# First channel product of batches 2 and 3 in eleven half-block products in place of twelve

## The chip, the cores and the metric

The kernel runs on one core of a Trainium2 chip, in one launch. The metric is the device time of one execution in microseconds (us). The core has TensorE (matrix products, written PE in the profile, with its weight loads as PEld), VectorE (DVE), ScalarE (ACT), GpSimd (POOL) and SyncE (SP), each with an instruction stream of its own that it works through in order; they wait for each other by semaphores. TensorE writes its results to `P`, the accumulation memory of 8 banks of 128 x 512 fp32 numbers; VectorE and ScalarE fetch them from there.

## The reference

Two stages, for 4 batches of 768 tokens and 8 heads of width 48 (together 384 channels). The first is a recurrence over the tokens of each head: the state S (48 x 48) gives y_t = q_t S, and then takes in beta_t k_t (v_t - S k_t), with k normed. The second is a mixer on x = y of all heads:

```
h = transpose(x) @ U @ V          (over the tokens, rank 32)
u = x + transpose(h)
out = u + max(u @ w_ch1, 0) @ w_ch2      (384 -> 1536 -> 384)
```

All is fp32. The inputs q, k, v, beta and the weights come as 64-bit floats and are converted on the chip.

## The kernel before

The recurrence is done in chunks of 64 tokens. Each batch has two units n of 6 chunks; a unit's triangular systems are solved on VectorE (`blocks`, a chain of pairs of operations at L596 and L602), and joined and applied by small products on TensorE (L505 to L888). Its outputs land in `X`.

The mixer of a batch is done in three groups i of 256 tokens (`GT`). `front(b, i)` adds the low-rank part for two tiles of 128 tokens (a product with `v_sb` at L1054, an add on VectorE at L1058) and turns each by three transposes (L1062) and a copy on ScalarE (L1065) into `ut`, channels by tokens. `wide(b, i)` is the first channel product: 12 blocks of 128 hidden channels, each the sum of 3 products of 128 x 128 weights with 256 tokens (L1132), two blocks to a bank, ending in one relu on ScalarE (L1088). In the same function follows the second channel product (L1169) in `PRODUCTS` = 7 products of sums in place of 8, each of six 128 x 192 blocks, with sums made by VectorE (`add_up` L1104, `last_sum` L1111) and gathered into `X` (L1117).

Two of the eight banks of `P` (names `mix`) serve the channel products and alternate; the other six, in pairs, serve everything else.

The order of all instructions is fixed when the kernel is built. Every piece of work is a generator (`op` yields one step with its engine and an expected cost, `need` what it waits for), and `run()`, the planner, plays all of them against a model of the engines' times: at each step it takes, per engine, the piece with the lowest place among those that can start soon (`hold`, L238). Places are given where a piece begins and are overruled by the list `PLACES`, so recurrence work is mixed with the channel products of the batch before. The framework then adds the semaphore waits that the tiles' reads and writes ask for, in the order in which the instructions were issued. So the model's costs set the order, and the built program sets who waits.

Of the kernel before, what the change touches and what calls it, by code (L numbers as in the profile page):

```python
# [16 lines left out]
BK = 32  # L17
# [9 lines left out]
def kernel(  # L27
# [42 lines left out]
    conv = ctx.enter_context(tc.tile_pool(name="conv", bufs=2))  # L70
# [70 lines left out]
    add_up b1 i0 15.701; block b0 i0 c0 64.5; block b0 i1 c2 71.091; block b0 i1 c3 56.313  # L141
    block b0 i2 c5 93.473; block b1 i0 c0 14.618; block b1 i0 c1 14.618; block b1 i1 c2 14.618
    block b1 i1 c3 14.618; block b1 i2 c4 14.618; block b1 i2 c5 14.618; block b2 i0 c0 93.5
    block b2 i0 c1 93.5; block b2 i1 c2 93.5; block b2 i1 c3 93.5; block b3 i0 c0 65.835
    block b3 i0 c1 65.835; block b3 i2 c4 65.835; block b3 i2 c5 65.835; blocks n0 1.5
    blocks n3 97.0; blocks n5 79.5; diagonals n1 h0 59.5; front b1 i0 79.5
    front b2 i0 58.8; gather b0 i0 h1 c0 70.591; gather b0 i1 h1 c0 70.591; gather b0 i1 h1 c1 70.591
    gather b1 i0 h1 c1 79.0; gather b1 i2 h1 c0 97.0; gather b2 i0 h0 c0 21.0; gather b2 i1 h1 c0 21.0
    gather b2 i1 h1 c1 21.0; grams n2 i0 81.482; grams n2 i1 89.482; grams n3 i0 20.0
    grams n5 i0 31.5; grams n5 i1 20.5; grams n7 i0 13.5; joins n1 h0 12.5  # L150
    joins n2 h0 -3.0; joins n2 h1 -3.0; joins n7 h0 106.5; joins n7 h1 102.5
    last_sum b0 i0 74.5; last_sum b2 i0 27.644; load n0 namev halves(0, 1) 74.591; load n1 namek halves(0, 1) 49.32
    load n1 nameq halves(0, 1) 49.32; load n1 namez halves(0, 1) 49.82; load n4 namek halves(0, 1) 86.5; load n7 namek halves(0, 1) 75.587
    load_beta u0 14.5; load_weights 68.5; norms n1 59.3; norms n2 81.804
    norms n7 91.523; outputs b0 c2 3.5; outputs b0 c4 76.5; outputs b0 c6 46.644
    outputs b0 c7 36.586; outputs b0 c9 90.5; outputs b1 c11 9.0; outputs b1 c5 57.185
    outputs b2 c0 37.5; outputs b2 c11 37.5; outputs b2 c5 37.5; outputs b3 c5 79.0
# [206 lines left out]
    def load(n, name, halves):  # L364
# [11 lines left out]
        for g in halves:  # L376
            if n >= NU and g:
                queue = nc.gpsimd
# [651 lines left out]
    def front(b, i):  # L1030
# [37 lines left out]
        for c in cs:  # L1068
            begin(block(c), 2)
# [10 lines left out]
    def wide(b, i):  # L1080
        yield need(("front", b, i), ("narrow", *before(b, i)))
        x, ut = X[:, b % 2], uts[b, i]
        if b == 0 and i == 0:
            yield ["mixing"]
# [146 lines left out]
```

## Time and profile before

| | us |
|---|---|
| median of 3 runs | 622.55 (621.05 to 623.77) |
| the profiled execution | 622.19 |
| its span from first to last instruction | 620.1 |
| TensorE busy | 589.1 (95%) |
| VectorE busy | 401.0 (65%) |
| ScalarE busy | 228.3 (37%) |
| first product L1132, 864 records | 201.9 |
| second product L1169, 1008 records | 176.1 |

A product of fp32 stands in the profile as two records, each a weight load (PEld) and a matmul (PE). Records overlap: a matmul's row lasts until its last result has left the array, while the next has begun. The pace is therefore read from the starts, or from the chain of waits, and not from the mean length of one. The chain of waits lists the work that ended last, step by step; what stands in it sets the end.

Batch 2's first group begins its first product at about 398 us, batch 3's at about 527 us. After 527 us TensorE has the mixer of batch 3 alone.

### The profile page before, as it was taken

The page shows a single profiled execution, that of the slowest core. Times are in us where ns is not written, and L with a number is a line of the kernel's source. Part 1 is how long each engine was busy: PE and PEld are TensorE (multiplying, and loading weights), DVE is VectorE, ACT ScalarE, POOL GpSimd, SP SyncE. Part 2 cuts the span into 40 slices and gives each one's busy share as a digit, 9 for nine tenths or more (in the row PEclk, how much of TensorE's full clock was granted, in tenths as well). Part 3 has the DMA queues.
Part 4 walks back from the last instruction along what each step waited for, and adds up shares of the span by engine and source line. Part 5 has one row for each costly group of instructions (what it writes and reads, how often), then busy time and mean ns, then how long its engine had stood idle before and what let it go on. Part 6 is the DMA issues. An engine that isn't in the chain of part 4 may idle for free.

```text
span 620.1 us, 23438 instructions
## 1 busy us (share of the span) xinstructions
PE 589.1 (95%) x10536; PEld 518.6 (84%) x10536; DVE 401.0 (65%) x965; ACT 228.3 (37%) x450; POOL 82.5 (13%) x145
## 2 busy tenths in 40 slices
PE   6678988999999999999999999999999999999997
PEld 5578976789888878799889878889889869898987
DVE  5869997898989613889898128898894123131312
ACT  3465564740342553521621643245324321101020
POOL 3011052410010343200100511401001000000000
PEclk9766565999999999999999999999999999999999
DMA  9840568850000332410000611600000000000000
GB/s 146 159 88 5 177 177 177 186 123 14 15 4 29 64 75 52 77 37 0 30 3 13 113 41 30 133 2 3 30 3 14 16 3 9 18 5 21 15 12 25
DMA packets 72004, 33.26 MB, mean 54 GB/s; under 512 B 59616, under 2 KB 70368, under 8 KB 71904
## 3 DMA queue, kind: packets, MB, share of 16 engines
q1 hardware_dynamic: 66112, 24.98, 18.3%
q0 software_dynamic: 4192, 6.49, 4.6%
q8 instruction: 82, 1.34, 0.9%
q10 hardware_dynamic: 1600, 0.30, 0.3%
q14 instruction: 18, 0.15, 0.1%
HBM read 27.03 MB, written 4.72 MB: 51 GB/s over the span
## 4 chain that ended last, share of the span: by engine, by line
PE 82%; DVE 9%; SPq 5%; issue 2%; DMA 1%; ACT 0%; ACTq 0%; DVEq 0%
PE P L1132 30%; PE P L1169 27%; SPq L382 4%; PE P L505 3%; PE P L478 2%; PE P L860 2%; PE P L1054 2%; PE P L775 2%; PE P L888 2%; PE P L811 2%; PE P L789 2%; DVE prod L596 1%; DVE xt L602 1%; PE P L822 1%; PE P L666 1%
## 5 line engine op out<-in xcount | busy, mean ns | idle before, releaser
L1132 PE MATMUL P<-ut,w_sb 128*128 128x256 f32 x864 | 201.9, 385 | 0.0
L1132 PEld LDWEIGHTS P<-ut,w_sb 128*128 128x128 f32 x864 | 159.4, 190 | 22.4 <-issue 0.6
L1169 PE MATMUL P<-w_sb,hs 128*128 128x192 f32 x720 | 125.6, 329 | 0.0
L1169 PEld LDWEIGHTS P<-w_sb,hs 128*128 128x128 f32 x720 | 117.1, 190 | 3.9 <-issue 1.2
L1088 ACT ACTIVATE hs<-P 128x512 f32<-128x512 f32 x72 | 43.0, 597 | 167.1 <-PE P L1132 163.1
L1117 DVE TENSOR_TENSOR X<-X,P 128x192 f32<-128x192 f32 x84 | 29.4, 350 | 62.7 <-PE P L1169 62.1
L602 DVE TENSOR_TENSOR xt<-xt,prod 128x112 f32<-128x112 f32 (+21 forms) x200 | 64.6, 323 | 6.9
L596 DVE TENSOR_TENSOR prod<-gs,xt 128x112 f32<-128x112 f32 (+21 forms) x200 | 64.1, 321 | 4.8
L759 ACT COPY X<-P 64x192 f32<-64x192 f32 x96 | 30.1, 313 | 71.3 <-PE P L789 54.6
L1169 PE MATMUL P<-w_sb,S 128*128 128x192 f32 x288 | 50.5, 329 | 0.0
L1169 PEld LDWEIGHTS P<-w_sb,S 128*128 128x128 f32 x288 | 46.8, 190 | 0.6
L1104 DVE TENSOR_TENSOR S<-hs 128x384 f32<-128x384 f32 x24 | 13.2, 552 | 52.4 <-ACT hs L1088 52.3
L873 DVE TENSOR_TENSOR z<-slot,P 128x192 f32<-128x192 f32 x44 | 15.5, 352 | 45.6 <-PE P L860 30.8
L478 PE MATMUL P<-ident,slot 128*128 128x128 f32 x192 | 30.4, 309 | 13.4 <-DMA slot<-in_k_dram 11.4
L478 PEld LDWEIGHTS P<-ident,slot 128*128 128x128 f32 x192 | 25.0, 158 | 18.3 <-issue 13.2
L731 ACT COPY slot<-zz 32x384 f32<-32x384 f32 x64 | 32.5, 509 | 12.2 <-DVE zz L609 7.9
L493 ACT COPY slot<-P 128x768 f32<-128x768 f32 x30 | 23.7, 803 | 31.1 <-PE P L478 30.9
L581 POOL MEMSET xt<- 128x1056 f32 x8 | 7.8, 980 | 186.7 <-DVE zz L609 186.7
L505 PE MATMUL P<-slot 48*64 48x64 f32 x1536 | 31.8, 238 | 0.5 <-ACT slot L493 0.2
L505 PEld LDWEIGHTS P<-slot 48*64 48x64 f32 x1536 | 28.7, 150 | 3.9 <-ACT slot L493 2.1
L738 POOL MEMSET slot<- 32x384 f32 x32 | 13.6, 424 | 108.6 <-PE P L695 63.0
L382 POOL DMA_DIRECT2D slot<-in_k_dram x36 | 24.2, 679 | 28.1 <-PE P L888 28.1
(119 smaller groups left out, 780.7 us busy)
## 6 DMA issues: line engine op xcount, KB each, us to landing
out_dram<-X SPq DMA_DIRECT2D x24, 192.0 KB, 1.9
slot<-in_k_dram SPq DMA_DIRECT2D x56, 72.0 KB, 4.0
X<-in_moe_w_ch_dram SPq DMA_DIRECT2D x10, 384.0 KB, 5.5
wide<-in_moe_w_ch_dram SPq DMA_DIRECT2D x10, 384.0 KB, 5.1
slot<-in_q_dram SPq DMA_DIRECT2D x40, 72.0 KB, 3.6
slot<-in_v_dram SPq DMA_DIRECT2D x40, 72.0 KB, 2.7
slot<-in_k_dram POOLq DMA_DIRECT2D x36, 72.0 KB, 3.9
slot<-in_q_dram POOLq DMA_DIRECT2D x24, 72.0 KB, 4.6
```

The source lines that it names most:

```text
L382: queue.dma_start(out=t[half(1 - g if name == "z" else g), :, to, 0:D], in_=src[b, 4 * g + s, hf * UC * L : (hf + 1) * UC * L, :].rearrang ...
L478: nc.tensor.transpose(p_t[:, c // 3, c % 3], t[:, c, 2 * j : 2 * j + 2].rearrange("p s d -> p (s d)"), ident,)
L493: nc.scalar.copy(to, p_t)
L505: nc.tensor.matmul(p_g[half(g ^ (par * i)), par, c], kq[rows, c, j, 0, half(g)], kq[rows, c, j, i, half(g)], start=True, stop=True,)
L596: nc.vector.tensor_tensor(out=prod, in0=gb[:, :, j : j + 1, j + 1 :].to_broadcast([128, split, m, w]), in1=xb[:, :, 0:m, j : j + 1].to_bro ...
L602: nc.vector.tensor_tensor(out=xb[:, :, 0:m, j + 1 :], in0=xb[:, :, 0:m, j + 1 :], in1=prod, op=ALU.subtract,)
L731: nc.scalar.copy(pg[quarter(i), :, at, :, a : a + BK], cut(zc, h)[quarter(i)].rearrange("p r (c j) t -> p r c j t", j=2),)
L759: nc.scalar.copy(x[half(c % 2), c // 2, 4 * D * g : 4 * D * (g + 1)].rearrange("p (j r d) -> p r j d", r=2, d=D), states(p_y)[half(g)],)
L1088: nc.scalar.activation(hs[:, fs[0] : fs[1] + 1 : fs[1] - fs[0]], p_f, ACTF.Relu)
L1117: nc.vector.tensor_tensor(out=to, in0=to, in1=p, op=ALU.add)
L1132: nc.tensor.matmul(p_f[:, fs.index(f)], w1_sb[:, y, 256 * t + 128 * fs.index(f) :][:, 0:128], ut[:, t], start=(t == 0), stop=(t == KT - 1),)
L1169: nc.tensor.matmul(p_o, a[:, f], w2_sb[:, w, f], start=(first and f == 0), stop=(f == HF - 1), skip_group_check=True,)
```

## The change

For the six groups of batches 2 and 3 (`QUICK` = (2, 0) and on) the first product is done another way. A pair is now a block f and the block f + 6 (`PAIRS`), and the 256 tokens are taken as two halves. Of the three channel tiles the first two make a 2 x 2 by 2 x 2 block product, which `seven` does in 7 products by sums of weights and of tokens; the third adds 4 plain ones. So a pair takes 11 products of 128 x 128 weights with 128 tokens, where it took 6 with 256.

- `weight_sums` makes, once, three tiles of weight sums in `w1_sums` and overwrites a part of `w1_sb` by a difference (four operations of 768 columns on VectorE).
- `token_sums` makes five 128-column sums for each group; one of them goes to the room of `beta_rows`.
- `seven` holds three running sums in the first 384 columns of one bank: px, pz and py. px is read three times in the course of the sum and goes on being added to, pz once. ScalarE copies px and pz to `hs` (`copies`), then px again (`copy_of`); VectorE adds py, pz and px to what was copied (`add`, `rest`); ScalarE's relu takes the last px. `cut_off` does the relu of the three other quarters on `hs`, for three pairs at once, and `add_up` waits for it.
- Batches 0 and 1 keep the old form (`plain`).
- `front` does two token tiles by one step each: two products, one add of 768 columns, six transposes, one copy.
- `hold` for low places is 0.18 in place of 0.5, the list `PLACES` is another, the pool `conv` goes (its room is taken from `w1_sums`), four small constants share a tile, `norms` uses single buffers, and the DMAs that GpSimd issues are booked to it.

```diff
@@ -235,7 +230,7 @@
-                    hold = 0.5 if i[0] < 13 else HOLD if i[0] < 90 else SWITCH
+                    hold = 0.18 if i[0] < 13 else HOLD if i[0] < 90 else SWITCH
...
@@ -287,7 +282,8 @@
 
     ident = const.tile([128, 128], FP32, name="ident")
     make_identity(nc, ident)
-    upper = conv.tile([128, 128], FP32, name="upper", tag="power", bufs=1)
+    w1_sums = const.tile([128, 3, FT // 2, 128], FP32, name="w1_sums")
+    upper = w1_sums[:, 0, 0]
...
@@ -372,10 +366,10 @@
             e = "sp" if halves == (0,) else "act"
         else:
             e = "sp"
-        queue = dict(sp=nc.sync, act=nc.scalar)[e]
         for g in halves:
             if n >= NU and g:
-                queue = nc.gpsimd
+                e = "pool"
+            queue = dict(sp=nc.sync, act=nc.scalar, pool=nc.gpsimd)[e]
             for s in range(1, 4, 2) if name == "z" else range(4):
                 to = dict(k=s, q=s, v=s % 2 * 2 + s // 2, z=s // 2)[name]
                 yield op(e, 0.65, port=False)
...
-    PAIRS = ((0, 1), (2, 6), (7, 8), (3, 4), (5, 9), (10, 11))
+    PAIRS = tuple((f, HF + f) for f in range(HF))
...
-            conv.tile([128, 2 * WIDE], I32, name="wide", bufs=1),
+            w1_sums.bitcast(I32).rearrange("p s f x -> p (s f x)")[:, 0 : 2 * WIDE],
-        uppers, powers = room[:, 2 * WIDE :], conv.tile([128, WIDE], I32, name="power", bufs=1)
+        uppers = room[:, 2 * WIDE :]
+        powers = w1_sums.bitcast(I32).rearrange("p s f x -> p (s f x)")[:, 2 * WIDE :]
...
@@ -1048,26 +1045,22 @@
         cs = list(range(i * GT // 128, (i + 1) * GT // 128))
         ut = uts[b, i] = mix.tile([128, KT, GT], FP32, name="ut")
-        def block(c):
-            o = yield op("pe", 0.65, "F", take="pair", words=4)
-            p_h = one(o)[:, 0:DM]
+        at = slice(cs[0], cs[-1] + 1)
+        o = yield op("pe", 1.3, "F", take="pair", words=8)
+        p_h = pair(o)[:, :, 0:DM]
+        for m, c in enumerate(cs):
             nc.tensor.matmul(
-                p_h, v_sb[:, c * 128 : (c + 1) * 128], tt, start=True, stop=True
+                p_h[:, m], v_sb[:, c * 128 : (c + 1) * 128], tt, start=True, stop=True
             )
-            yield op("dve", dve(384), give=[("pair", o)])
-            nc.vector.tensor_tensor(out=x[:, c], in0=x[:, c], in1=p_h, op=ALU.add)
-            o = yield op("pe", 0.56, "F", take="pair", words=6, flow=0.32)
-            p_u = one(o)[:, 0:DM].rearrange("p (t n) -> p t n", t=KT)
+        yield op("dve", dve(768), give=[("pair", o)])
+        nc.vector.tensor_tensor(out=x[:, at], in0=x[:, at], in1=p_h, op=ALU.add)
+        o = yield op("pe", 0.84, "F", take="pair", words=12, flow=0.64)
+        p_u = pair(o)[:, :, 0:DM].rearrange("p m (t n) -> p m t n", t=KT)
+        for m, c in enumerate(cs):
             for t in range(KT):
-                nc.tensor.transpose(p_u[:, t], x[:, c, t * 128 : (t + 1) * 128], ident)
-            at = c * 128 - i * GT
-            yield op("act", act(384), give=[("pair", o)])
-            nc.scalar.copy(ut[:, :, at : at + 128], p_u)
-            emitted(("ut", b, c))
-
-        for c in cs:
-            begin(block(c), 2)
-        yield need(*[("ut", b, c) for c in cs])
+                nc.tensor.transpose(p_u[:, m, t], x[:, c, t * 128 : (t + 1) * 128], ident)
+        yield op("act", act(768), give=[("pair", o)])
+        nc.scalar.copy(ut.rearrange("p t (m n) -> p m t n", m=NT), p_u)
         emitted(("front", b, i), 0.1)
     def reserve():
...
@@ -1077,9 +1070,55 @@
         free["mix"].update({0: state["now"], 1: state["now"]})
         emitted("mixing")
+    QUICK = (2, 0)
+    def weight_sums():
+        w = w1_sb.rearrange("p y (t k x) -> p y t k x", t=KT, k=2)
+        a11, a12, a21, a22 = w[:, :, 0, 0], w[:, :, 1, 0], w[:, :, 0, 1], w[:, :, 1, 1]
+        n1, s2, s4 = (w1_sums[:, z] for z in range(3))
+        b, i = before(*QUICK)
+        yield need(("weights", W2 + 5), ("narrow", *before(b, i)))
+        yield op("dve", dve(768), port=True)
+        nc.vector.scalar_tensor_tensor(
+            out=n1, in0=a21, scalar=-1.0, in1=a22, op0=ALU.mult, op1=ALU.subtract
+        )
+        yield op("dve", dve(768), port=True)
+        nc.vector.scalar_tensor_tensor(
+            out=s2, in0=n1, scalar=-1.0, in1=a11, op0=ALU.mult, op1=ALU.subtract
+        )
+        yield op("dve", dve(768), port=True)
+        nc.vector.tensor_tensor(out=s4, in0=a12, in1=s2, op=ALU.subtract)
+        yield need(("wide", b, i))
+        yield op("dve", dve(768), port=True)
+        nc.vector.tensor_tensor(out=a21, in0=a11, in1=a21, op=ALU.subtract)
+        emitted(("w1 sums", 0), 0.1)
+    sums_of = {}
+    def token_sums(b, i):
+        yield need(("front", b, i), ("wide", *before(b, i)), ("w1 sums", 0))
+        ut = uts[b, i]
+        u = ut.rearrange("p t (m n) -> p t m n", m=2)
+        ts = mix.tile([128, 3, 128], FP32, name="ts", bufs=1)
+        rest = beta_rows.rearrange("p b t -> p (b t)")
+        for to, a, c, how in (
+            (ts[:, 0], u[:, 0, 0], u[:, 0, 1], ALU.subtract),
+            (ts[:, 1], u[:, 1, 1], ts[:, 0], ALU.add),
+            (ts[:, 2], u[:, 1, 0], ts[:, 1], ALU.subtract),
+            (u[:, 0, 1], u[:, 1, 1], u[:, 0, 1], ALU.subtract),
+            (rest, u[:, 2, 0], u[:, 2, 1], ALU.subtract),
+        ):
+            yield op("dve", dve(128), port=True)
+            nc.vector.tensor_tensor(out=to, in0=a, in1=c, op=how)
+        sums_of[b, i] = ts[:, 0], ts[:, 1], ts[:, 2], rest
+        emitted(("tokens", b, i), 0.1)
     def wide(b, i):
         yield need(("front", b, i), ("narrow", *before(b, i)))
         x, ut = X[:, b % 2], uts[b, i]
+        quick = (b, i) >= QUICK
         if b == 0 and i == 0:
             yield ["mixing"]
...
@@ -1094,6 +1133,7 @@
         def add_up(f0, fs):
             yield need(*[("h", b, i, x) for x in fs])
+            yield need(*[("cut", b, i, e, f0) for e in (0, 3, 1)]) if quick else []
             at = slice(f0, f0 + 3)
             for to, a, c, how in (
                 (S1[:, at], part(0, 1, f0), part(1, 1, f0), ALU.add),
...
@@ -1121,26 +1161,126 @@
                 nc.sync.dma_start(out=out[b, at : at + 128, :], in_=x[:, NT * i + c])
                 emitted(("stored", b, NT * i + c), 2.0)
...
+        w1 = w1_sb.rearrange("p y (t k x) -> p y t k x", t=KT, k=2)
...
+        def seven(y):
+            t1, t2, t4, t5 = sums_of[b, i]
+            n1, s2, s4 = (w1_sums[:, z, y] for z in range(3))
+            def u(t, m):
+                return ut[:, t, 128 * m : 128 * m + 128]
+            def mm(to, w, t, start=False, stop=False):
+                nc.tensor.matmul(to, w, t, start=start, stop=stop, skip_group_check=True)
+            def c(k, m):
+                return part(k, m, y, 1)[:, 0]
+            m = yield op("pe", 0.433, "F", take="mix", words=8)
+            p_of = mixed(m).rearrange("p (z n) -> p z n", n=128)
+            px, pz, py = (p_of[:, z] for z in range(3))
+            mm(px, w1[:, y, 0, 0], u(0, 0), start=True)
+            mm(pz, n1, t1)
+            def add(e, k, m, p):
+                yield op("dve", dve(128), rush=True)
+                nc.vector.tensor_tensor(out=c(k, m), in0=c(k, m), in1=p, op=ALU.add)
+                emitted(("c", b, i, e, y), 0.06)
+            def copies():
+                yield op("act", act(256), rush=True)
+                of = hs.rearrange("p f (m n) -> p (f m) n", m=2)
+                nc.scalar.copy(of[:, 2 * y : 2 * (HF + y) + 2 : 2 * HF + 1], p_of[:, 0:2])
+                emitted(("begun", b, i, y), 0.06)
+                yield need(("other", b, i, y))
+                yield from add(0, 0, 0, py)
+            begin(copies(), 3)
+            yield op("pe", 0.433, "F", words=8)
+            mm(py, w1[:, y, 1, 0], u(1, 0))
+            mm(py, w1[:, y, 2, 0], u(2, 0), stop=True)
+            emitted(("other", b, i, y), 0.22)
+            yield need(("begun", b, i, y))
+            yield op("pe", 0.217, "F", words=4)
+            mm(px, s2, t2)
+            def copy_of():
+                yield op("act", act(128), rush=True)
+                nc.scalar.copy(c(0, 1), px)
+                emitted(("second", b, i, y), 0.06)
+            begin(copy_of(), 3)
+            yield op("pe", 0.433, "F", words=8)
+            mm(pz, s4, u(1, 1))
+            mm(pz, w1[:, y, 2, 0], u(2, 1), stop=True)
+            emitted(("both", b, i, y), 0.22)
+            def rest():
+                yield need(("both", b, i, y), ("second", b, i, y))
+                yield from add(1, 0, 1, pz)
+            begin(rest(), 3)
+            yield need(("second", b, i, y))
+            yield op("pe", 0.433, "F", words=8)
+            mm(px, w1[:, y, 0, 1], u(0, 1))
+            mm(px, w1[:, y, 2, 1], u(2, 1))
+            yield from add(3, 1, 1, px)
+            yield op("pe", 0.433, "F", words=8)
+            mm(px, w1[:, y, 1, 1], t4)
+            mm(px, w1[:, y, 2, 1], t5, stop=True)
+            emitted(("all", b, i, y))
+            yield op("act", act(128), rush=True)
+            nc.scalar.activation(c(1, 0), px, ACTF.Relu)
+            emitted(("c", b, i, 2, y), 0.06)
+            yield need(*[("c", b, i, e, y) for e in (0, 1, 3)])
+            free["mix"][m] = state["now"] + 0.06
+        def cut_off(e, y):
+            k, m = divmod(e, 2)
+            yield need(*[("c", b, i, e, x) for x in range(y, y + 3)])
+            yield op("act", act(384))
+            of = part(k, m, y)
+            nc.scalar.activation(of, of, ACTF.Relu)
+            emitted(("cut", b, i, e, y), 0.06)
+            if e == 0:
+                emitted(("h", b, i, PAIRS[y + 2]))
+        def eleven():
+            yield need(("tokens", b, i), ("w1 sums", 0))
+            for y in range(HF):
+                begin(seven(y), 94)
+                if y % 3 == 2:
+                    for e in (0, 3, 1):
+                        begin(cut_off(e, y - 2), 3)
+                    begin(add_up(y - 2, ()), 4)
+            yield need(("all", b, i, HF - 1))
+        if quick:
+            yield from eleven()
+        else:
+            yield from plain()
         emitted(("wide", b, i))
         begin(last_sum(), 4)
...
-            (0, part(0, 0, 0, HF), [("h", b, i, x) for x in ((3, 4), (5, 9))] + [("weights", W2 + 2)],
+            (0, part(0, 0, 0, HF), [("h", b, i, PAIRS[x]) for x in (2, 5)] + [("weights", W2 + 2)],
-            (1, part(1, 0, 0, HF), [("h", b, i, (10, 11)), ("weights", W2 + 5)], 1, True, 0, 0, False),
+            (1, part(1, 0, 0, HF), [("weights", W2 + 5), *[("c", b, i, 2, x) for x in range(HF) if quick]],
+             1, True, 0, 0, False),
...
+        begin(weight_sums(), 50)
+        for b in range(B):
+            for i in range(NG):
+                if (b, i) >= QUICK:
+                    begin(token_sums(b, i), 3)
```

## The prediction

> **What bounds the kernel now.** I read the page's engine lines and slices first, then the chain of waits over the last 80 us, then the groups by shape, then two stretches of the timeline. On the page TensorE is busy 95% of the span, and its clock is full from 120 us on:
>
> ```profile
> PE 589.1 (95%) x10536; PEld 518.6 (84%) x10536; DVE 401.0 (65%) x965; ACT 228.3 (37%) x450; POOL 82.5 (13%) x145
> PE   6678988999999999999999999999999999999997
> PEclk9766565999999999999999999999999999999999
> ```
>
> The chain of waits from 540 us on is TensorE alone, with no gap between pieces. One first product (L1132) of a group takes 15.54 us for its 72 records (216 ns each), one second product (L1169) 13.65 us for 84 (162.5 ns each). So 1 us of TensorE work, or 1 us of TensorE waiting, is 1 us of the end.
>
> ```profile
> 546.84 11.70 PE P L1169 x72
> 558.55 15.54 PE P L1132 x72
> 574.09 13.65 PE P L1169 x84
> 587.74 15.54 PE P L1132 x72
> 603.28 13.66 PE P L1169 x84
> 616.94 0.02 issue
> 616.97 0.35 DVE X L1117
> ```
>
> The groups by shape: a product of fp32 is two records, each a weight load and a matmul. L1062 is the transposes, the only 128-wide records with a 128-column load.
>
> ```profile
> L1132 PE MATMUL P<-ut,w_sb 128*128 128x256 f32 x864 | 201.9, 385 | 0.0
> L1169 PEld LDWEIGHTS P<-w_sb,hs 128*128 128x128 f32 x720 | 117.1, 190 | 3.9 <-issue 1.2
> L1062 PE MATMUL P<-ident,X 128*128 128x128 f32 x72 | 10.7, 276 | 0.0
> L1062 PEld LDWEIGHTS P<-ident,X 128*128 128x128 f32 x72 | 8.3, 141 | 0.8 <-DVE X L1058 0.2
> ```
>
> The timeline of that place (columns: start, length, what) gives the pace of a 128-wide record:
>
> ```profile
> 546.03 0.82 PE L1062 MATMUL P<-ident,X 128*128 128x128 f32 x6
> 546.57 1.93 PEld L1169 LDWEIGHTS P<-w_sb,hs 128*128 128x128 f32 x12
> 546.68 2.12 PE L1169 MATMUL P<-w_sb,hs 128*128 128x192 f32 x12
> ```
>
> Six transposes start at 546.03 and the next product at 546.68: 0.65/6 = 109 ns each. The last record's end lies 0.82 - 0.65 = 0.17 us after that: a result can be read 0.17 us after the array has gone on. The load at 546.57 is of the fp32 kind (190 ns in its row), and its matmul starts 0.11 us later, in pace.
>
> What a wait costs that nothing covers is seen at 501 us, where TensorE ran out of other work:
>
> ```profile
> 501.05 0.45 PE L860 MATMUL P<-s,slot 48*64 48x48 f32 x16
> 501.63 0.35 DVE L873 TENSOR_TENSOR z<-slot,P 128x192 f32<-128x192 f32 x1 [1.59 <-PE P L860]
> 502.04 0.27 PEld L888 LDWEIGHTS P<-z,slot 64*48 64x48 f32 x16 [0.20 <-DVE z L873]
> ```
>
> The matmuls end at 501.50, VectorE starts 0.13 later (at 616.94 the same step took 0.03), and TensorE's load starts 0.06 after VectorE's end. A full load then stands before the first 128-column matmul, 0.11 us. So a round trip costs 0.17 + 0.03 + the operation + 0.05 + 0.11 = **0.36 us plus the operation**, 0.46 at most.
>
> **The change, part by part.**
>
> *TensorE work.* Per weight pair six 256-wide products become eleven 128-wide ones: 12 records of 216 ns = 2.59 us become 22 of 109 = 2.40 us. Over 36 pairs (six groups of six): 36 x 0.19 = **7.0 us less**. The pace of a 128-wide fp32 record in a row is in no trace; its bounds are 107 ns (half of 216) and 190 ns (if the load's recorded length were the pace: 4.18 us a pair, 57 us more). I take 109, because the fp32 load at 546.57 was hidden behind a 128-wide matmul.
> The Trainium skill ("TensorE: Matmul & The Clock Gate", Part 3, "What overlaps and what doesn't") speaks against it: loads overlap running matmuls only where the row groups differ, and here all use all rows. By its load of 128/1.2 = 107 ns (an estimate from that page) a record would take 216 ns, and the change would cost 36 x 2.16 = 78 us on this term. The trace contradicts it: L1169's loads use all rows and last 190 ns, at a pace of 162.5.
>
> *The new waits.* This is the term that decides. The three running sums px, pz and py of a pair lie in one bank of `P`, and the planner books a wait only where the same sum is read and then continued. In the order of the changed program, with the semaphore that each instruction waits for, the waits are by bank. With a1..a11 the products of `seven` in the order issued: a3 (py) waits for `copies` (which reads px and pz), a6 (pz) for `copy_of` (px), a8 (px) for the add of py, a10 for the adds of pz and px. The planner holds a3-a4 and a6-a7 for the cover of these very reads; they stand behind the waits themselves. TensorE runs in order, so what could cover is only what is issued between. In a group with nothing else (the last two) the order is a1-a2, a3-a5, a6-a7, a8-a9, then a1-a2 of the next pair in the other bank, a10-a11, and so on. The operations' lengths come from these rows:
>
> ```profile
> L700 ACT COPY zz<-P 128x192 f32<-128x192 f32 x16 | 5.1, 319 | 3.8 <-PE P L695 3.6
> L1065 ACT COPY ut<-P 128x384 f32<-128x384 f32 x24 | 10.7, 486 | 24.1 <-PE P L1062 17.9 <-DVE X L1117 5.3 <-DVE s L898 1.0
> L1117 DVE TENSOR_TENSOR X<-X,P 128x192 f32<-128x192 f32 x84 | 29.4, 350 | 62.7 <-PE P L1169 62.1
> L602 DVE TENSOR_TENSOR xt<-xt,prod 128x126 f32<-128x126 f32 x6 | 1.7, 290 | 0.2
> ```
>
> ACT gains 0.87 ns a column between 192 and 384, so 128 columns take 0.26 and 256 take 0.375 us. A 128-wide add takes 0.29 (126 columns; from PSUM at most the 0.35 of 192). Per pair:
> - a6 behind `copy_of`, nothing between: 0.36 + 0.26 = 0.62.
> - a8 behind the add of py, nothing between: 0.36 + 0.29 = 0.65.
> - a10 behind two adds with 0.04 between them: 0.36 + 0.62 = 0.98, less four records (0.44) of the next pair: 0.54.
> - a3 behind `copies`, 0.36 + 0.375 = 0.73: covered by a10-a11 and their wait, except in a group's first pair.
>
> That is 1.81 us a pair against 0.19 saved. For a group: 6 x 1.81 + 0.73 at the head + 0.44 at the foot (no next pair) - 0.4 where pairs four and five are issued crosswise = 11.6 us. I went along the issued order of the others in the same way, setting each round trip against the TensorE work between (recurrence pieces by their chain times, 0.2 to 0.9 us): batch 3's first group 9.0 (copy and add in one trip of 0.95 in three pairs), batch 2's second 10.8, its first 7.8 and its third 3.2, where recurrence and state products stand between. Sum: 7.8 + 10.8 + 3.2 + 9.0 + 11.6 + 11.6 = **54.0 us more**, over 88 exposed waits. Behind a waiting instruction all of TensorE's queue stands, and VectorE's adds, which wait for TensorE, hold back the substitution pairs (L596, L602) queued behind them in batch 2. With 0.46 a trip and 0.35 an add it would be some 65 us, with 0.28 a trip 47.
> The bank rule has a reason in the Trainium skill ("PSUM — Partial Sum Buffer", Terms): two engines in one bank and quadrant at once are an error. No run here shows a bank read while it is written; by columns alone two of the four waits would shrink to about 0.2 us each, and the sum would be near 630.
>
> *VectorE and ScalarE elsewhere.* `weight_sums` (four adds of 768, 0.95 each by L1111's 949 ns, 3.8 us) runs ahead of batch 2's first group; VectorE is busy 4.3 and 8.3 of 20 us there (340 to 380 us), so nothing. If that cover were gone, 3.8. `token_sums` (5 x 0.29 = 1.5 us a group) runs beside the second product before it (13.65 us, VectorE at 7 x 0.35 + 2.6): nothing. ScalarE's new 0.26 + 0.375 + 0.26 + 0.49 = 1.4 us a pair is under the pair's 4.2: nothing beyond the waits counted.
>
> *Fronts by two tiles.* TensorE's records are the same. VectorE's add (0.95) and the trip (0.36) make 1.31 us between value product and transposes; six second products (1.95 us) stand between in most, 0.87 in one: 0.4 us more.
>
> *The new plan.* Places and hold change, so everything is reordered, DMA issues on SP and POOL too (the 84 DMAs that POOL issued before as well are now booked to it, and no longer to SP). TensorE issues 1298 instructions before the first group (1358 before) and 4136 before batch 2's (4040): 96 small matmuls come earlier, about 2 us, and are missing as cover later. TensorE idles 24 us in the first 120 us (windows of 20 us: 96 busy), so a better or worse front could be worth some 6 us either way; I take 0.
>
> **Sum** against the profiled execution's own 622.19 us (span 620.1, 2.1 around it; the median is 0.4 above): 622.2 - 7.0 + 54.0 + 0.4 = **669.6, say 670 us**.
>
> **The rivals.**
> - *The other bank covers the waits* (the other side): two pairs are open at once, so TensorE would always have work. For it: two banks. Against it: the order above. Then 622.2 - 7.0 + 0.4 = 616. It decides where less than 0.19 us a pair stays exposed; I count 1.5. Chance 0.03.
> - *Half of the waits are covered* by recurrence, or trips are shorter (0.2 us): 622 - 7 + 27 = 642. Chance 0.08.
> - *The load sets the pace* (190 ns): 36 x 22 x 0.081 = 64 more, less 0.32 a pair at a10: 670 + 64 - 12 = 722. Against it: 546.57. Chance 0.05.
> - *The clock halves*, since TensorE works only 2.4 of 4.2 us in a pair; at 20 to 112 us it fell to 0.5 and 0.6 with busy shares of 65 to 96%, but on small tiles. For it: records of 213 ns in the 24 pairs of the four groups with little cover, 24 x 22 x 0.104 = 55: 725. Against it: at 491 to 505 us, with exposed waits, it stayed 1.0. Chance 0.06.
>
> **How the numbers follow.** The forecast (waits exposed at 0.36 a trip, full clock) has 0.78. Its own range by the bounds of trips, adds and front: 655 to 690. The range for 8 in 10 reaches to the half-covered case: 645 to 695. A change of 0.5% (3 us) is what a measurement can tell from none; only the first rival, and a part of the second with a better front, ends within or below it: faster 0.03, same 0.01, slower 0.96.
>
> **What would show it.** In the profile after: the new product's 792 records at a pace of 109 ns where unbroken; its weight loads idle before ScalarE's copy and VectorE's add as releasers, in sum some 50 us; last groups of 25 to 26 us for 15.5 before, second products still 13.7; chain shares of VectorE and ScalarE up by some 5% together; ScalarE's copies of 128 columns near 0.26, adds near 0.29; clock 1.0 to the end. It would be wrong if releasers of these loads were few, if records stood 190 apart, or if the clock fell after 400 us.

## The result, and the profile after

The changed kernel takes 678.54 us (median of four runs, 676.78 to 681.02) against 622.67 us (621.05 to 623.77) for the kernel before on the same chip: a ratio of 1.0909, 95% interval 1.0883 to 1.0935. The profiled execution of after took 676.78 us, with a span of 675.1 us (620.1 before).

These are the engine line, two rows of slices and the chain's shares of the page of after:

```profile
PE 604.2 (90%) x10896; PEld 532.8 (79%) x10896; DVE 436.0 (65%) x1095; ACT 252.7 (37%) x546; POOL 83.8 (12%) x145
PE   4697877999999999999999988898898997978878
PEclk9758677999999999999999998999999999999999
PE 75%; DVE 10%; ACT 5%; SPq 4%; issue 3%; DMA 3%; DVEq 0%; ACTq 0%
```

TensorE's row of nines ends just ahead of batch 2's first group. ScalarE, which was at 0% of the chain, now holds 5% of it. TensorE shows 15.1 us more busy time than before although it has less to do, since after a wait the end of a matmul's row no longer lies under the next record: the same 132 records of a group are busy 19.56 us here and 14.63 us in a run without the waits (below). Busy time is no measure of work here; the stretches are. From the start of batch 2's first group, in windows (stretch, its length, busy us and records of each engine, granted clock, DMA share, GB/s), first of before:

```profile
398.42:509.49 111.07, 110.35 (x2105) 94.74 (x2104) 73.95 (x187) 42.13 (x88) 6.04 (x13) 1.00 0.07 18
509.49:527.25 17.76, 17.76 (x107) 16.63 (x106) 6.36 (x14) 2.32 (x5) 0.00 (x0) 1.00 0.03 11
527.25:602.90 75.65, 75.65 (x395) 69.54 (x394) 15.82 (x34) 11.01 (x19) 0.00 (x0) 1.00 0.04 14
```

and of after (batch 2, then the three first-product groups of batch 3):

```profile
406.33:551.39 145.06, 132.12 (x2188) 118.50 (x2187) 76.54 (x217) 54.04 (x138) 4.27 (x8) 0.99 0.05 13
551.39:575.85 24.46, 19.28 (x136) 16.37 (x136) 6.53 (x23) 7.92 (x23) 0.00 (x0) 1.00 0.03 9
592.22:618.19 25.97, 19.56 (x133) 16.04 (x132) 6.39 (x22) 7.53 (x23) 0.00 (x0) 1.00 0.02 9
631.96:657.93 25.97, 19.56 (x132) 16.04 (x132) 6.40 (x22) 7.53 (x23) 0.00 (x0) 1.00 0.03 9
```

So of the 55.0 us of span, 7.9 lie ahead of batch 2 (398.42 to 406.33), 16.2 in batch 2 (128.83 to 145.06) and 30.9 in batch 3 (92.85 to 123.71 up to the end).

The lines of the changed kernel that matter are L1176 (plain first product), L1310 (second product), L1196 (the eleven products), L1215 (`copies`), L1231 (`copy_of`) and L1209 (the adds). The chain of waits of after in the last group (start, length, what) shows the greater part of one pair of blocks:

```profile
634.00 0.27 ACT hs L1231
634.27 0.04 issue
634.31 0.73 PE P L1196 x4
635.04 0.03 issue
635.07 0.02 DVEq L1209
635.09 0.04 issue
635.13 0.30 DVE hs L1209
635.43 0.04 issue
635.48 0.73 PE P L1196 x4
636.20 0.02 issue
636.22 0.50 DVE hs L1209 x2
```

Where before had one piece of 15.54 us of TensorE, TensorE and the reader of its bank now take turns: two products, a copy or an add, two products. Four records take 0.73 us here. The groups by shape give the readers' lengths and what ended TensorE's idle time (the first row has only the products of `ut` and `w_sb`):

```profile
L1196 PE MATMUL P<-ut,w_sb 128*128 128x128 f32 x432 | 71.1, 287 | 16.8 <-DVE hs L1209 9.2 <-ACT hs L1215 4.2 <-ACT hs L1231 2.9
L1209 DVE TENSOR_TENSOR hs<-hs,P 128x128 f32<-128x128 f32 x108 | 28.3, 286 | 98.4 <-PE P L1196 72.6 <-ACT hs L1231 16.2 <-ACT hs L1215 9.5
L1215 ACT COPY hs<-P 128x256 f32<-128x256 f32 x36 | 13.2, 371 | 73.9 <-PE P L1196 73.8
L1231 ACT COPY hs<-P 128x128 f32<-128x128 f32 x36 | 9.5, 265 | 32.1 <-PE P L1196 26.9 <-DVE hs L1209 5.1
```

The weight loads of all eleven products stood idle behind these readers for 43.0 us in 77 waits (us in all, times, longest), 27.2 us of it in batch 3 and 15.9 in batch 2:

```profile
PEld P L1196 <- DVE hs L1209: 22.2, 43, 0.9
PEld P L1196 <- ACT hs L1231: 14.3, 24, 0.9
PEld P L1196 <- ACT hs L1215: 6.5, 10, 0.7
```

### The profile page after: what moved, and what is told of

Its sections match the earlier page's. It is cut to its first block, busy times and chain, and to the rows that moved or that the text cites. A ratio compares the mean times of both kernels' runs of the same rounds, so it can differ in the third digit from the quotient of the medians.

```text
span 675.1 us, 24368 instructions
## 1 busy us (share of the span) xinstructions
PE 604.2 (90%) x10896; PEld 532.8 (79%) x10896; DVE 436.0 (65%) x1095; ACT 252.7 (37%) x546; POOL 83.8 (12%) x145
## 4 chain that ended last, share of the span: by engine, by line
PE 75%; DVE 10%; ACT 5%; SPq 4%; issue 3%; DMA 3%; DVEq 0%; ACTq 0%
PE P L1310 25%; PE P L1196 16%; PE P L1176 14%; SPq L376 3%; PE P L501 3%; DVE hs L1209 3%; PE P L474 2%; PE P L1052 2%; PE P L856 2%; PE P L818 1%; PE P L884 1%; ACT hs L1231 1%; DMA w_sums<-in_moe_w_ch_dram 1%; PE P L807 1%; PE P L771 1%
## 5 line engine op out<-in xcount | busy, mean ns | idle before, releaser
L1310 PE MATMUL P<-w_sb,hs 128*128 128x192 f32 x720 | 125.2, 328 | 0.0
L1310 PEld LDWEIGHTS P<-w_sb,hs 128*128 128x128 f32 x720 | 116.7, 190 | 2.8 <-issue 0.6
L1176 PE MATMUL P<-ut,w_sb 128*128 128x256 f32 x432 | 102.2, 386 | 0.0
L1209 DVE TENSOR_TENSOR hs<-hs,P 128x128 f32<-128x128 f32 x108 | 28.3, 286 | 98.4 <-PE P L1196 72.6
L1176 PEld LDWEIGHTS P<-ut,w_sb 128*128 128x128 f32 x432 | 79.3, 190 | 11.1
L1196 PE MATMUL P<-ut,w_sb 128*128 128x128 f32 x432 | 71.1, 287 | 16.8 <-DVE hs L1209 9.2
L1196 PEld LDWEIGHTS P<-ut,w_sb 128*128 128x128 f32 x432 | 57.1, 192 | 24.6 <-DVE hs L1209 12.8
L1310 PE MATMUL P<-w_sb,S 128*128 128x192 f32 x288 | 50.0, 328 | 0.0
L1310 PEld LDWEIGHTS P<-w_sb,S 128*128 128x128 f32 x288 | 46.8, 190 | 0.6
L474 PE MATMUL P<-ident,slot 128*128 128x128 f32 x192 | 31.9, 319 | 15.2 <-DMA slot<-in_k_dram 6.7
L1127 ACT ACTIVATE hs<-P 128x512 f32<-128x512 f32 x36 | 21.5, 597 | 57.9 <-PE P L1176 57.3
L474 PEld LDWEIGHTS P<-ident,slot 128*128 128x128 f32 x192 | 26.7, 165 | 18.5 <-issue 14.9
L1215 ACT COPY hs<-P 128x256 f32<-128x256 f32 x36 | 13.2, 371 | 73.9 <-PE P L1196 73.8
L1196 PE MATMUL P<-ts,w_sums 128*128 128x128 f32 x144 | 28.8, 282 | 1.1 <-DVE hs L1209 0.7
```

The source lines that it names most:

```text
L474: nc.tensor.transpose(p_t[:, c // 3, c % 3], t[:, c, 2 * j : 2 * j + 2].rearrange("p s d -> p (s d)"), ident,)
L1176: nc.tensor.matmul(p_f[:, k], w1[:, y, t, k], ut[:, t], start=(t == 0), stop=(t == KT - 1),)
L1196: nc.tensor.matmul(to, w, t, start=start, stop=stop, skip_group_check=True)
L1209: nc.vector.tensor_tensor(out=c(k, m), in0=c(k, m), in1=p, op=ALU.add)
L1310: nc.tensor.matmul(p_o, a[:, f], w2_sb[:, w, f], start=(first and f == 0), stop=(f == HF - 1), skip_group_check=True,)
```

## The experiments

The theory on trial: a pair's three running sums in one bank make TensorE and the readers take turns, and this is where the time went. The rival: the new plan (places, hold, fronts) costs it. All twelve runs were timed beside the kernel before (medians 622.34, 622.80 and 621.55 us in the three sets). "Group" is the time from the first to the last record's start of one first product in batch 3; in the kernel before it is 15.3 us.

### The waits alone, behind an equal plan

Four kernels with the places and the hold of before. The first has plain products throughout (`QUICK` is (4, 0), and no weight sums), the others eleven products in batch 3 alone:

```
-    QUICK = (2, 0)
+    QUICK = (3, 0)
```

> The changed kernel with plain products in all batches (no weight sums, no token sums) and with the kernel before's table of places and its hold of 0.5; what is left of the change is the fronts by two token tiles, the new order of the pairs, the released buffers. It asks why the changed kernel with plain products took 644.9 us and not 622. Theory: the new places and the hold of 0.18 are made for longer groups in batch 2 and leave batch 3's recurrence without products beside it; with the old ones it is 622 to 626 us, and the recurrence of batch 3 has products of batch 2 beside it as in the kernel before. Rival: the fronts by two tiles or the buffers upset the plan themselves: 635 us or more, again with a stretch of recurrence alone at a granted clock of 0.5 ahead of batch 3's first front.

> As the run with the old places and hold, but with the eleven products in batch 3 alone, all sums of a pair in one bank as in the change. Nothing but the three groups differs behind batch 2, and no recurrence is left there to cover, so the waits should show in full. Theory (waits by bank on the path): groups of 26 us for 15.5, so 3 x 10.5 = 31.5 us over the run with plain products, about 655 us if that is 623. Rival (the cost is the plan's and not the waits'): under 635 us.

> As the run before this one in the list (eleven products in batch 3 alone, old places), but leaving out the copies, the second copy and the three adds of each pair: three of the four quarters of the hidden tile of batch 3 are not made anew. TensorE's 22 products a pair stay. Theory: groups of 14.6 us, 0.9 less than plain, so 3 x 0.9 = 2.7 us under the run with plain products, about 620 us if that is 623: this is all that one product in twelve is worth here. Rival: without cover elsewhere in the plan this is lost as in the run with all four quarters unread in batches 2 and 3 (644 us): 630 us or more.

> Eleven products in batch 3 alone, old places, each running sum in a bank of its own (three banks a pair, two pairs at a time) and the planner told that a product waits for the read before it, with the trip to and fro, so that two pairs run in turn. Theory: each wait of 0.62 to 0.73 us has 0.43 us of the other pair's products and 0.43 of its own in front of it, but for the last (add, then two products), which leaves 0.2 to 0.3 us a pair, and the handing over of the banks some 0.7 us for two pairs: 14.6 + 6 x 0.25 + 2 x 0.7 = 17.5 us a group, 3 x 2 = 6 us over plain, about 629 us. Rival (the waits can be hidden altogether): 15 us a group and 621 us, under the kernel before.

The last three differ from each other as follows (an excerpt; third kernel: no reads, the second copy and the other adds go in the same way; fourth: banks, and the planner told):

```
-            begin(copies(), 3)
+            emitted(("begun", b, i, y))
+            emitted(("c", b, i, 0, y))
...
-            p_of = mixed(m).rearrange("p (z n) -> p z n", n=128)
+            if b < LAST:
+                p_of = mixed(m).rearrange("p (z n) -> p z n", n=128)
+            else:
+                p_of = P[:, 2 + m :: 2, 0:128]
...
+                yield need(("p", b, i, y, 2))
                 yield op("act", act(128), rush=True)
```

Measured: plain 649.92 us (ratio 1.0426, 1.0377 to 1.0475); one bank 677.66 (1.0895, 1.0848 to 1.0942); no reads 642.76 (1.0325, 1.0287 to 1.0362); three banks and told 647.02 (1.0400, 1.0352 to 1.0448). The windows of batch 3's groups, in this order, plain first:

```profile
588.08:603.40 15.32, 15.32 (x72) 13.49 (x72) 1.94 (x4) 2.98 (x5) 0.00 (x0) 1.00 0.04 15
```

one bank:

```profile
550.70:576.93 26.23, 19.66 (x133) 16.04 (x132) 6.48 (x22) 7.76 (x23) 0.00 (x0) 1.00 0.03 9
592.64:618.83 26.19, 19.66 (x133) 16.04 (x132) 6.48 (x22) 7.76 (x23) 0.00 (x0) 1.00 0.03 9
632.59:658.78 26.19, 19.66 (x133) 16.04 (x132) 6.49 (x22) 7.75 (x23) 0.00 (x0) 1.00 0.03 9
```

no reads:

```profile
550.72:565.35 14.63, 14.63 (x134) 14.63 (x132) 1.94 (x4) 3.97 (x11) 0.00 (x0) 1.00 0.05 16
581.06:595.68 14.62, 14.62 (x132) 14.62 (x132) 1.94 (x4) 3.85 (x11) 0.00 (x0) 1.00 0.05 16
609.45:624.08 14.63, 14.63 (x133) 14.63 (x133) 2.49 (x5) 3.85 (x11) 0.00 (x0) 1.00 0.05 16
```

three banks, planner told:

```profile
547.96:565.33 17.37, 16.39 (x133) 15.23 (x132) 7.12 (x22) 7.29 (x22) 0.00 (x0) 1.00 0.04 14
581.04:596.81 15.77, 15.77 (x133) 15.18 (x132) 7.12 (x22) 7.20 (x22) 0.00 (x0) 1.00 0.04 15
610.58:627.84 17.26, 16.39 (x133) 15.22 (x133) 7.13 (x22) 7.20 (x22) 0.00 (x0) 1.00 0.04 13
```

The kernels with one bank and with no reads begin batch 3 at 550.70 and 550.72 us, so all that differs is behind that point: three groups of 78.61 against 43.88 us, 34.7 us, and 34.9 us between the medians. The reads cost 11.6 us a group, 1.93 us a pair, and all of it is time of the kernel. This settles the theory for batch 3. It also gives the worth of the arithmetic. From the start of one group's first product to the next group's, with a second product between, the run without reads takes 28.39 us (581.06 to 609.45) and the plain kernel 29.19 (588.08 to 617.27): 0.8 us a group, some 5 us in six, an estimate since only three were measured. With three banks and the planner told most of the waiting is gone, yet the groups are still 0.5 to 2 us longer than plain ones.

The plain kernel begins batch 3 at 556.94 us and the fourth at 547.96, so with these two the groups may be compared but not the totals. All four totals missed their expectations, by 24, 23, 23 and 18 us, mostly for one reason: with the old places, the plain kernel is 27 us slower than the kernel before, all of it ahead of batch 3. The rival named for that run won, and the plan became the second question.

### Banks and planner in the changed kernel

Three banks a pair in batch 3; the planner told in both batches; both together; and the reads left out in both. The lines that tell the planner of the first wait are (an excerpt):

```
+                yield need(("p", b, i, y, 1))
                 yield op("act", act(256), rush=True)
...
+            emitted(("p", b, i, y, 1), 0.22)
             begin(copies(), 3)
+            yield need(("begun", b, i, y))
             yield op("pe", 0.433, "F", words=8)
```

> In batch 3 alone px, pz and py of a pair lie in three banks (six banks for the two open pairs; the recurrence has ended by then). Theory (waits are exposed because the sums share a bank): the waits before a3 and a6 go, a8 waits for the copy alone (0.62 less 0.44 = 0.18), a10 for one add (0.65 less 0.44 = 0.21): groups of 14.4 + 6 x 0.4 + 0.7 = 17.5 us in place of 26.1, the kernel at 678 - 3 x 8 = 654. Rival (the waits are the sums' own, whatever the bank, or 128-wide records are slow in themselves): groups stay at 26, the kernel at 678.

> The same products and banks; the planner is told of the waits by bank (a3 for the copies, a6 for the second copy, a8 for the adds of py and pz, and 0.22 us from product to reader, 0.16 us back), so that the two open pairs run in step, each in the other's waits. Theory: per two pairs 0.30 before a3, 0.54 before a8, 0.21 before a10 and 0.18 for the bank's release stay open, 0.6 a pair in place of 1.8: groups of 14.5 + 3.7 = 18.2 us, the kernel at 678 - 4 x 8 - 4 = 642 us. Rival (the other bank's pair does not run while one waits, or it is not the waits): groups stay near 26, the kernel at 670 or more.

> The changed kernel with eleven products in both batches, batch 3's running sums in three banks a pair, and the planner told of the wait for each read in both batches. Theory: batch 3's groups of 16 to 17.5 us as in batch 3 alone, for 18.6 in one bank with the planner told and 18.2 to 19.4 in three banks without; so 4 to 6 us under 652 us, 646 to 648, and still above the kernel before, since 14.6 us is the least that 22 products a pair take and the plan around them is late. Rival: hiding more of the waits gives batch 3's recurrence less cover, and the time stays at 652 or goes up.

> The eleven products without ScalarE's two copies and VectorE's three adds in their course; only the last relu of px is read. So three of four quarters of the hidden channels are not made anew, and the output is not the reference's. Theory (TensorE's work is 1.2 us a group less, the waits are all of the loss): groups of 66 products at 0.219 = 14.5 us plus at most 0.7 at the ends, the kernel at 622 + 8 - 7 = 623 us. Rival (the weight load sets the pace at 190 ns a record, or the 128-wide form loses elsewhere): groups of 20 us and more, the kernel above 650.

| | us | ratio (95%) | groups of batch 3, us | batch 2, us |
|---|---|---|---|---|
| the change | 678.54 | 1.0909 (1.0883 to 1.0935) | 24.5, 26.0, 26.0 | 145.1 |
| three banks | 658.24 | 1.0584 (1.0539 to 1.0628) | 19.4, 18.2, 18.7 | 144.1 |
| told | 652.21 | 1.0467 (1.0421 to 1.0513) | 22.6, 18.6, 18.6 | 135.7 |
| three banks, told | 647.21 | 1.0409 (1.0376 to 1.0441) | 19.2, 15.8, 17.3 | 136.2 |
| no reads | 644.21 | 1.0355 (1.0314 to 1.0396) | 14.6, 14.6, 14.6 | 143.6 |

"Batch 2" is from its first group's start to batch 3's. In batch 3 the groups fall as the theory says: separate banks alone take 5 to 8 us off a group, an order that leaves room for the round trip 2 to 7. That fits the Trainium skill ("PSUM — Partial Sum Buffer", Summary: rules for kernel authors), which says that a bank to be read while matmuls run should be another than theirs; the 26.0 and 18.2 us of the second group are its price here. The kernel with the planner told missed its 642 us by 10, the one with three banks its 654 by 4; the two together fell into their range, though their first group (19.2 us) did not.

The run without reads missed its 623 us, and where it missed is the lesson: batch 2 took 143.6 us without a single one of the waits, only 1.5 less than with them (and 14.8 more than before). Two windows of it, from batch 2's first group on:

```profile
409.83:501.80 91.97, 91.96 (x1468) 88.24 (x1467) 51.51 (x133) 35.68 (x83) 1.64 (x4) 1.00 0.03 11
501.80:553.42 51.62, 40.75 (x727) 34.33 (x726) 13.45 (x32) 8.51 (x19) 2.61 (x4) 0.70 0.08 21
```

Batch 2's first products were used up at 502 us, TensorE had been full until then, and in the next 51.6 us batch 3's recurrence had only batch 2's last second product (13.67 us) beside it, at a mean granted clock of 0.70. Read this way, the waits in batch 2 had been partly beside that recurrence, and taking them away moves idle time from one place to another. This is not shown: leaving the reads out changed the planner's order too (batch 2 begins at 409.83 us for 406.33), and one wait of 5.1 us in that stretch is for a load of v, as in the plain kernel below. A plan that knows of the waits gets 9 us of batch 2 back; what the 7 us over before's 128.8 are that stay, no run separates.

### The plan

Plain products in the changed kernel with its own new places and hold; the old places and fronts by single tiles; the kernel before with nothing but the new fronts; and the changed kernel with one group of joins moved.

```
-    QUICK = (2, 0)
+    QUICK = (4, 0)
...
             es = [12 * r + 2 * c + j for r, c in spots for j in range(2)]
+            yield need(("tokens", 2, 0)) if n == 6 else []
```

The first line is the plain kernel's, the last the moved joins'; the new fronts alone are those of the change's diff (one add of 768 and one copy of 768 for two of 384 each).

> All of the change but the eleven products: batches 2 and 3 keep the plain first product, the fronts by two tiles, the new places and the smaller hold stay. Theory (the waits by bank in the eleven products carry 47 us of the 55, the seam ahead of batch 2 the other 8): 622 + 8 = 630 us, or less where the plan without the eleven products fills that seam; each first product with nothing beside it back at 15.54 us. Rival (the new plan and the fronts carry much of the loss): above 640 us.

> As the changed kernel with plain products in all batches, old places and old hold (649.9 us), but with the fronts by single token tiles as in the kernel before. If the fronts by two tiles are what upsets the old table of places, this comes back to 622 to 628 us; if any other of the small edits (pairs of blocks, one-buffer norms, further needs) does it as well, it stays at 635 us or more.

> The kernel before with one part of the change alone, the fronts by two token tiles; places, hold, products, pairs are those of before. Theory of the prediction: their own cost is +0.4 us in all, so 623 us if the planner's order stays about the same. Rival: the order is found by a planner whose table of places fits one list of requests only, and any change in the requests costs more than the request itself: 635 us or more, lost in batches 0 and 1 (batch 2's first group at 410 us or later for 398), and this, not the fronts' instructions, is why the changed kernel with plain products and the old places took 650 us.

> The changed kernel, with one need more: the joins of batch 3's first unit (those that stand in TensorE's queue at 401 us ahead of the second transposes of batch 2's first front) may be planned only after that front's token sums. Theory: the 7.9 us that the changed kernel starts late with batch 2's first group of products (406.3 against 398.4 us) are those transposes waiting behind joins that wait for two transposes on VectorE; with the joins behind, the group starts at 399 to 401 us, the granted clock stays at 1.0 there, and the kernel takes about 671 us for 678.5. Rival: what is late is VectorE itself with the weight sums and the front's add: the start stays at 405 us or later, and the time at 677 or above.

Measured: plain with the new places 644.86 us (1.0364, 1.0328 to 1.0400), where 630 was expected and the rival said above 640; fronts by single tiles with the old places 641.06 (1.0307, 1.0273 to 1.0341); new fronts alone 667.45 (1.0739, 1.0706 to 1.0772); joins moved 680.71 (1.0944, 1.0908 to 1.0980).

The new fronts alone made the kernel before 46 us slower, though TensorE's records are the same and VectorE's and ScalarE's are fewer and longer. The longest wait of that kernel's TensorE between 231 and 304 us (what waited for what: us in all, times, longest):

```profile
PE P L860 <- DVE slot L536: 25.1, 1, 25.1
```

and its windows from batch 0's last group to batch 1's first and from batch 2's last to batch 3's first:

```profile
231.36:303.48 72.12, 44.83 (x1179) 37.48 (x1177) 44.43 (x109) 22.78 (x46) 11.02 (x19) 0.81 0.13 30
531.61:572.26 40.65, 33.89 (x672) 28.87 (x671) 10.34 (x24) 7.86 (x19) 0.82 (x2) 0.83 0.04 12
```

One masking (L536) stands in VectorE's queue behind a whole unit's substitution pairs, and TensorE waits 25.1 us for it. Before had 37.9 us from the end of batch 0's last group to batch 1's first, this kernel 72.1. These two stretches are 34 and 23 us longer than before, the others together some 11 shorter. It is not the fronts' own instructions: in another order of the queues nearly the same work is 46 us dearer. The list of places fits one list of requests. The kernel with single-tile fronts and the old places is better than with the new fronts (641 for 650), but not back at 622, so the other small edits upset the list too. Which of them was not tried.

Plain products under the new places lose most of their time in the same place as the run without reads, between batch 2's last first product and batch 3's first. Its TensorE between 494 and 550 us:

```profile
PE P L818 <- DVE slot L457: 6.0, 1, 6.0
PE P L856 <- DVE s L894: 2.2, 4, 0.6
```

and its windows:

```profile
400.30:494.06 93.76, 93.74 (x1244) 82.62 (x1243) 48.36 (x120) 28.91 (x56) 2.56 (x5) 1.00 0.04 12
494.06:549.79 55.73, 43.68 (x972) 36.59 (x971) 17.13 (x36) 16.27 (x34) 4.25 (x8) 0.76 0.08 20
```

A load of v is issued only at 512.5 us, L457 waits for it until 519.9, and the recurrence then runs with nothing beside it. (The new places were made for the eleven products, so what they cost with plain ones is not what they cost in the change.) In the kernel before only 17.8 us lie between batch 2's last first-product group and batch 3's first, here 55.7.

The joins in front of batch 2 were the wrong suspect. With them out of the way the stretch from batch 1's last group to batch 2's first fell from 33.95 to 30.47 us (27.32 before) and the granted clock no longer dropped, but the group behind it grew from 36.34 to 38.96 us, and the kernel is not faster. From the front's add to the first product there are still 5.8 us (400.98 to 406.80): transposes, copy and token sums one after the other, where the kernel before had a second product between. VectorE's queue had a transpose of 2.11 us (L605, from 402.86) ahead of the first token sum and the second front's add (0.95 us) ahead of the others, which fits a part of the rival named for this run. This part of the 7.9 us is not settled further.

No version beat the kernel before. Of the 55 us of the change, the 30.9 in batch 3 are shown to be the waits, less the work saved there; the 16.2 in batch 2 and the 7.9 ahead of it hold waits and order together, and no run separates them. Without any wait at all, and in a plan as good as the old one, the change would be worth some 5 us (0.8%, estimated from the 0.8 us a group).

## Why the prediction was right, and where it was not

The time, its sign and the deciding term held: 669.6 us was the sum for the profiled execution, 676.78 came. Term by term:

- **The new waits, +54.0 us.** For batch 3 mechanism and size held: 32.2 us of waits were forecast, and leaving the reads out gave back 34.7. Of 88 waits 77 stand in the trace, with 43.0 us of idle weight loads where some 50 were to be seen. Of the round trips, `copy_of` measures 0.03 + 0.27 + 0.04 + 0.28 = 0.62 us (forecast 0.62), where the 0.28 is four records in 0.73 us for 0.45 in pace; the add of py, by the same rows, 0.72 (forecast 0.65). The operations were taken as 0.26, 0.375 and 0.29 us and measure 0.265, 0.371 and 0.286.
- **The same term in batch 2, 21.8 us of the 54.0.** The stretch grew by 16.2 us where waits less saved work made 18.3. The number fits, the reason is not shown. The waits are there (15.9 us of idle loads: 4.7, 9.3 and 1.9 in its groups, where 7.8, 10.8 and 3.2 us were forecast), but without the reads only 1.5 us came back, with a planner that knows of them 9. The step in doubt is setting each trip against the TensorE work beside it as if the stretch were TensorE's own; its length may also be that of batch 3's recurrence, which has to be covered. That the number came out is in part luck.
- **TensorE work, -7.0 us.** Mis-sized: a 128-wide record goes at 111.7 ns (14.63 us over 131 steps) and not 109, and a group saves 0.8 us and not 1.14. That is 5 us in six groups. (The prediction calls L1062 the only records of that form; L478 has 192 more, 12 of them in 1.31 us at 393 us, the same 109 ns.) The bound of 190 ns is out: the loads still last 192 ns in their row and are hidden.
- **The new plan, taken as 0 with 6 us either way.** This is most of what the sum lacked: 7.9 us ahead of batch 2, of which 6.6 lie between the last plain group and the first of eleven. Its bound was wrong in kind. It was worked out from TensorE's idle time in the first 120 us, and the runs moved by 19 to 46 us when requests changed while the list of places did not. The change came with a list of its own; whether that kept its plan from being worse was not tried.
- **VectorE's sums, "nothing".** Three of the four weight sums did run beside other work at 347 to 351 us. The token sums of the first group did not: no second product stood there, and in the kernel with the joins moved they are in the 5.8 us above.
- **Fronts, +0.4 us.** Not measured: alone they cost 46 us by the order they brought about, which says nothing of their own price.
- **The rivals.** The other bank did not cover the waits, because TensorE's order put the next product of the same bank first. The clock did not halve in batch 3's groups; at the start of batch 2's first it was 0.50 for 3.4 us (405.76 to 409.17), which the prediction had named as a sign against itself, and which is too short to carry the rival's 55 us.

## What to carry to other kernels

Sums that are read while others of the same bank go on belong in banks of their own, and the order has to leave a round trip of 0.6 to 0.7 us between a product and the next in that bank; otherwise saving one product in twelve costs more than ten times what it brings (11.6 us a group for 0.8). In a kernel whose order was found by a planner for one list of requests, price an edit of the requests by what the order may do (here up to 46 us), and look at the in-order queue of the helping engine, not at its busy share. And a stretch that matches in size is not yet explained: leave the suspected wait out and see whether the time comes back.

## What the hardware showed that was not expected

The granted clock changed in steps of about 3.4 us, and it did not go by TensorE's busy share alone. In the one-bank groups above it stayed at 1.00 with TensorE busy 19.66 of 26.2 us (75%). In the last group of the kernel with the joins moved, 3.41 us at 60%, with waits of 0.35 to 0.6 us between full-size products, were followed by 3.41 us at half clock:

```profile
657.96:661.37 3.41, 2.03 (x14) 1.46 (x13) 0.77 (x3) 1.27 (x4) 0.00 (x0) 1.00 0.00 0
661.37:664.78 3.41, 3.41 (x13) 3.41 (x13) 1.59 (x3) 0.73 (x3) 0.00 (x0) 0.50 0.01 2
```

In the changed kernel with three banks, 3.41 us at 54%, many of its records on small tiles, were not:

```profile
405.42:408.83 3.41, 1.83 (x85) 1.68 (x73) 0.70 (x4) 1.38 (x4) 1.35 (x4) 1.00 0.02 5
408.83:412.24 3.41, 3.41 (x77) 3.13 (x80) 0.29 (x1) 3.17 (x7) 0.00 (x0) 1.00 0.01 2
```

And in the plain kernel under the new places:

```profile
512.00:519.00 7.00, 2.38 (x102) 2.00 (x101) 2.04 (x4) 1.60 (x2) 2.61 (x4) 0.98 0.48 115
519.00:526.00 7.00, 4.70 (x176) 4.57 (x176) 1.36 (x1) 2.01 (x3) 0.00 (x0) 0.53 0.01 2
526.00:529.00 3.00, 1.71 (x80) 1.33 (x80) 1.29 (x4) 0.70 (x3) 0.00 (x0) 0.99 0.00 0
529.00:549.40 20.40, 16.57 (x281) 11.29 (x282) 4.12 (x10) 3.93 (x11) 0.00 (x0) 0.50 0.01 2
```

The low clock follows the light stretch at 512 us, where TensorE waited 6.0 us. It came again at 529 after waits of no more than 0.6 us each, and stayed for 20 us of recurrence tiles of 48 and 64 rows and the front's products. TensorE's 81% there do not compare with the other shares, because a record lasts longer at half clock (16 records of L856 take 0.45 us at 527.39 and 0.68 at 529.27). The Trainium skill ("TensorE: Matmul & The Clock Gate", Part 1, "What's actually happening") puts the step down after one idle window of about 3.4 us; that agrees with the first drop here and would not foresee the one at 529 or the one at 661, if idle means without work. What decides was not tried, nor what half clock costs: ahead of batch 2 the change's drop of 3.4 us went with the joins that were moved, and the kernel was no faster.
